# Narrower one-hots in the second column of a strip, and five small moves in the order of work, in a spectral transform with balanced expert assignment

## The chip, the cores and the metric

The kernel runs on one core of a Trainium2 chip. The metric is the time of one execution on the device in microseconds (us). Three runs of the kernel before gave 534.44, 532.58 and 536.25 us, median 534.44. The profile comes from one further execution, whose span from the first to the last instruction is 534.3 us.

## The reference

Two stages follow one another. The first takes the real part of a two-dimensional Fourier transform of every batch; the second sends each of the 19968 rows to one of eight experts, with at most 2496 rows for each, and puts it through that expert's two matrices.

```python
# x: (8, 2496, 256)
X = np.fft.fft(np.fft.fft(x, axis=1), axis=2).real      # -> 19968 rows of 256
logits = rows @ w_gate                                  # 19968 x 8
for idx in np.argsort(-logits.flatten()):               # best (row, expert) pairs first
    tok, e = idx // 8, idx % 8
    if assigned[tok] >= 0 or counts[e] >= 2496: continue
    assigned[tok] = e; counts[e] += 1
for e in range(8):                                      # w1: 256x1024, w2: 1024x256
    out[assigned == e] = np.maximum(rows[assigned == e] @ w1[e], 0) @ w2[e]
```

## The kernel before

A program in which the order of instructions on TensorE (PE), VectorE (DVE), ScalarE (ACT) and GpSimd (POOL) is the order in which the Python code emits them. Four stretches follow each other.

**Load and logits (0 to about 100 us).** Each batch `b` is loaded (`a_t`, and its mirror image `b_t`) and folded on VectorE. Its columns are transposed on TensorE in three groups (`turn_x`), copied to SBUF by ScalarE, multiplied with a gate table (`gate_x`), and put in place (`place_y`).

```python
for b in range(B):
    a_t, b_t = ab.pop(b)
    nc.vector.tensor_tensor(a_t[:, :, :, 1:D], a_t[:, :, :, 1:D], b_t[:, :, ::-1, D - 1:0:-1], op=AL.add)
    nc.vector.tensor_tensor(a_t[:, :, :, 0], a_t[:, :, :, 0], b_t[:, :, ::-1, 0], op=AL.add)
    # ... loads; two more VectorE operations that write zball[b] for the transform ...
    zts[b] = [turn_x(b, pv, 0), turn_x(b, pv, 1)]       # eight transposes each, one copy
    if b > 0:
        gate_x(b - 1, zts.pop(b - 1))
    zts[b].append(turn_x(b, pv, 2))                     # four transposes
    if b > 0:
        low_y = place_y(b - 1)
    # ... tables of sines and cosines ...
low_y()
gate_x(B - 1, zts.pop(B - 1))
place_y(B - 1)()
```

After it the logits of all rows are computed with tables in two halves (`lps`), and the expert with the greatest logit of each row is chosen.

**Transform (about 100 to 172 us).** Forty units, two for each of twenty blocks of 128 x 8 rows, each of ten matmuls into a PSUM bank (`fftps`). A first search for the threshold of each expert (`first_chain`) goes on at the same time on VectorE. `yield` gives the estimated cost of what was emitted, `SYNC` means that a matmul follows which needs VectorE's result; the loop below puts units in between by these estimates. Four times a whole expert's first matrix is turned (`turn_w`).

```python
def turn_w(e, eng=None):
    for j in range(2):
        for fh in range(2):
            wps = big_ps("wps")                         # one of three PSUM banks, shared with fftps
            # two 512-wide matmuls into wps
            take(w1t[e][:, j, fs], wps, eng=eng)        # copy, here on ScalarE
    if e + 2 < E:
        load_w1(e + 2)

def unit():
    cost = next(units, None)
    if cost is not None:
        clock["PE"] += 1.15; clock["D"] += cost; clock["n"] += 1
        if clock["n"] in (18, 22, 28, 34):
            turn_w((18, 22, 28, 34).index(clock["n"]), "A")
            clock["PE"] += 2.0
    return cost is not None
```

A finished block is combined by VectorE into `stage` (`combine`: two additions, then copies on ScalarE and GpSimd, then a write to DRAM).

**Strips.** Rows that are sure of their expert are sorted straight into strips: each call (`sort_call`) takes eight columns of 128 rows as four pairs. A pair fills 24 slots for each of 8 experts (`SW` = 24, `EW` = 8 x 24 = 192). The second column of a pair counts on from where the first one stopped. The one-hots come from VectorE (`sort_mark`), the sort is a matmul.

```python
# in first_strips, t3 = slot in the strip, t1 = expert
nc.vector.tensor_scalar(v_i, in0=v, scalar1=-MARK, scalar2=0.0, op0=AL.add, op1=AL.max)
# ...
nc.vector.scalar_tensor_tensor(has, in0=t3, scalar=float(SW), in1=sure, op0=AL.is_lt, op1=AL.mult)
nc.vector.scalar_tensor_tensor(v, in0=t1, scalar=float(SW), in1=t3, op0=AL.mult, op1=AL.add)
nc.vector.scalar_tensor_tensor(spot, in0=v, scalar=1.0, in1=has, op0=AL.add, op1=AL.mult)

# in sort_mark(n)
for f in range(8):
    nc.vector.tensor_scalar(marks[n][:, f, 0:EW + 1], in0=rampw[:, 0:EW + 1], scalar1=spot[:, c:c + 1],
                            scalar2=None, op0=AL.is_equal)

# in sort_call(n, gs)
for g in gs:
    sps = big_ps("sps")
    for cc in range(2):
        for j2 in range(2):
            nc.tensor.matmul(sps[:, j2 * EW:(j2 + 1) * EW], lhsT=xl[:, 2 * g + cc, j2 * P:(j2 + 1) * P],
                             rhs=pt[:, 2 * g + cc, 0:EW], start=(cc == 0 and j2 == 0),
                             stop=(cc == 1 and j2 == 1))
    take(dst[:, :, 4 * u + g, :], sps[:, 0:2 * EW]...)  # one copy of 384 columns
```

Rows that are not sure, or find no slot, are left over; they are settled later and gathered.

**Experts (about 172 us to the end).** 56 tiles: 40 early ones from the strips (tiles 0 to 39), 16 late ones whose rows GpSimd gathers from DRAM. Each tile has three parts. In a part TensorE computes three (or two) blocks of the hidden layer (`hps`, two matmuls each, copied to `hb` by ScalarE or VectorE) for this tile, and one output block (`ops`, eight matmuls) for the tile before, which GpSimd writes to DRAM by row number. The rest of the assignment (`settle_rest`) is emitted in small steps after each part:

```python
def pace(j):                                            # after every part
    credit[0] = min(credit[0] + 1.9, CREDIT)            # CREDIT = 3.0
    while credit[0] > 0.0 and not placed:
        c = next(todo, "end")
        if c == "end":
            settled(j); return
        if c is SYNC:                                   # a pause: go on after the next part
            return
        credit[0] -= c

def settle_rest():
    yield from settle()                                 # ends in: yield SYNC; transpose of trun on TensorE
    for _ in range(NROUND - 1):
        yield from round_steps(4, 2)
    # ...
    yield from choose_rest()                            # choose(False); yield SYNC; count() on TensorE
    yield from slots(rest, LB)
    # ... then lists of the rows left over, and settled
```

When all is placed, `feed` (in part 1 of each tile) lets the gathers start, spread over the tiles that are left:

```python
while m < len(late) and placed and j >= min(max(placed[0] + 1 + m * (51 - placed[0]) // 15, 0 if m < 8 else 32), 38 + m):
    gather(late[m])                                     # three indirect DMAs issued by GpSimd
    m += 1
```

## Time and profile before

Busy time in some stretches, in us:

| stretch (us) | length | TensorE | VectorE | ScalarE | GpSimd | what runs |
|---|---|---|---|---|---|---|
| 60 to 80 | 20 | 12.29 | 18.73 | 16.84 | 7.35 | last folds |
| 100 to 120 | 20 | 17.70 | 17.90 | 8.47 | 11.10 | transform |
| 120 to 140 | 20 | 16.44 | 15.79 | 11.42 | 6.40 | transform |
| 160 to 180 | 20 | 17.95 | 17.14 | 15.61 | 5.22 | transform to first tile |
| 200 to 220 | 20 | 19.99 | 17.92 | 16.30 | 11.31 | early tiles |
| 300 to 350 | 50 | 49.50 | 31.04 | 31.70 | 27.48 | early tiles, gathers from 328 |
| 400 to 450 | 50 | 50.00 | 25.91 | 26.68 | 38.09 | early and late tiles |
| 500 to 534 | 34 | 23.92 | 11.03 | 11.22 | 22.10 | last tiles, last writes |

In the lines of a timeline that follow, the columns are: start in us, length in us, engine, line of the kernel, operation, what is written and read, its partitions and elements and type, how many in a row, and in brackets the idle time of the engine before it and what ended it. In a line of the stretches they are: the stretch, its length, then busy time and number of instructions of PE (matmuls), PEld (weight loads), DVE, ACT and POOL, the mean granted clock of TensorE as a share of full speed, the share of the DMA engines and their GB/s. GpSimd's busy time covers only part of what an indirect DMA costs it: about 0.97 us of length and 0.30 us of a gap that is there each time.

### The profile page before, as it was taken

The numbers are of one execution on the slowest core, as the hardware profiler recorded it, in microseconds if no ns is written. First come the engines' busy times: TensorE is split into PE (matmuls) and PEld (weight loads), VectorE is DVE, ScalarE is ACT, GpSimd is POOL, SyncE is SP. The second block draws the span as 40 slices with busy tenths as digits, with TensorE's granted clock in tenths as the row PEclk, the third lists the DMA queues.
The fourth block names the chain that finished last, engine by engine and source line by source line (L and its number), as shares of the span: only waits on it lengthen the run. The fifth ranks groups of instructions, "written<-read, shape, count | busy, mean of one in ns | idle before, by whom it ended". The sixth has DMA issues, their size and how long they took to land.

```text
span 534.3 us, 11232 instructions
## 1 busy us (share of the span) xinstructions
PE 471.8 (88%) x4039; PEld 357.7 (67%) x4039; DVE 372.7 (70%) x952; ACT 337.9 (63%) x762; POOL 313.9 (59%) x362
## 2 busy tenths in 40 slices
PE   0567659899789899999899999999999999999983
PEld 0544436776568566777667877777777777777753
DVE  7799994687978969889978757566654555555431
ACT  7879983156368778788767776556555555555531
POOL 7888815253122555555524336777677777777774
PEclk9968898999989999999989999999999999999988
DMA  8999929078578697523322323342222222222221
GB/s 259 317 281 319 310 89 159 2 240 291 140 217 261 161 225 163 137 95 103 99 76 100 99 88 102 113 130 85 82 83 78 79 87 84 79 69 78 77 77 53
DMA packets 35168, 74.62 MB, mean 140 GB/s; under 512 B 6115, under 2 KB 14349, under 8 KB 35104
## 3 DMA queue, kind: packets, MB, share of 16 engines
q0 software_dynamic: 23296, 42.10, 30.2%
q1 hardware_dynamic: 11808, 31.73, 17.7%
q8 instruction: 33, 0.54, 0.4%
q14 instruction: 31, 0.25, 0.2%
HBM read 51.26 MB, written 32.24 MB: 156 GB/s over the span
## 4 chain that ended last, share of the span: by engine, by line
PE 70%; DVE 13%; ACT 9%; issue 4%; DMA 3%; POOL 1%; POOLq 0%; DVEq 0%; ACTq 0%
PE hps L1234 24%; PE ops L1257 24%; PE sps L1098 5%; PE fftps L1038 5%; PE wps L1058 2%; PE tp L285 2%; ACT zt L287 2%; DMA xa<-in_x_dram 2%; PE yps L295 1%; ACT tf L254 1%; POOL out_dram L1261 1%; DVE xa L343 1%; PE inv_ps L766 1%; DVE stage L1022 1%; PE tp L1222 1%
## 5 line engine op out<-in xcount | busy, mean ns | idle before, releaser
L995 ACT ACTIVATE hb<-hps 128x384 bf16<-128x384 f32 (+1 forms) x326 | 146.2, 493 | 50.5 <-PE hps L1234 47.4
L1257 PE MATMUL ops<-w2t,hb 128*128 128x256 bf16 (+1 forms) x1344 | 175.3, 274 | 0.0
L1257 PEld LDWEIGHTS <-hb 128*128 128x128 bf16 (+1 forms) x1344 | 133.3, 100 | 32.6 <-issue 0.5
L1261 POOL DMA_INDIRECT out_dram<-zball,rid x85 | 89.3, 1051 | 82.7 <-ACT zball L995 63.8
L1234 PE MATMUL hps<-xs,zball 128*128 128x384 bf16 x640 | 127.3, 327 | 0.0
L1234 PEld LDWEIGHTS <-zball 128*128 128x128 bf16 x896 | 86.1, 98 | 43.4 <-issue 2.9
L999 DVE TENSOR_SCALAR hb<-hps 128x384 bf16<-128x384 f32 (+1 forms) x122 | 66.3, 549 | 47.2 <-PE hps L1234 39.2
L129 POOL DMA_INDIRECT xb<-in_x_dram,mir_i x40 | 54.3, 1357 | 11.9 <-issue 10.5
L995 ACT ACTIVATE zball<-ops 128x256 f32<-128x256 f32 (+1 forms) x79 | 30.4, 384 | 31.6 <-PE ops L1257 29.0
L1234 PE MATMUL hps<-xt,zball 128*128 128x384 bf16 (+1 forms) x256 | 48.4, 322 | 0.0
L285 PE MATMUL tp<-identf,xa 128*128 128x128 f32 x160 | 27.4, 336 | 20.1 <-issue 9.2
L285 PEld LDWEIGHTS tp<-identf,xa 128*128 128x128 f32 x160 | 23.6, 176 | 27.1 <-issue 10.2
L995 ACT ACTIVATE xs<-sps 128x384 bf16<-128x384 f32 x68 | 30.4, 493 | 16.0 <-PE sps L1098 15.7
L1026 POOL COPY stage<-stage 128x258 bf16<-128x258 bf16 x40 | 17.7, 447 | 36.3 <-DVE stage L1021 33.0
L1098 PE MATMUL sps<-pt,xl 128*128 128x192 bf16 x320 | 33.8, 246 | 0.7 <-DVE pt L1076 0.7
L1076 DVE TENSOR_SCALAR pt<-rampw,spot 128x193 bf16<-128x193 bf16 x160 | 32.5, 298 | 1.6 <-PE inv_ps L766 0.9
L1098 PEld LDWEIGHTS <-xl 128*128 128x128 bf16 x320 | 27.6, 98 | 3.5 <-issue 1.6
L1210 POOL DMA_INDIRECT xg<-t_dram,ids_l x24 | 23.1, 964 | 7.3 <-issue 7.3
L1261 POOL DMA_INDIRECT out_dram<-zball,rows_l x23 | 22.3, 969 | 7.3 <-issue 2.4
L1044 ACT COPY ev<-fftps 128x512 f32<-128x512 f32 x20 | 11.7, 584 | 22.9 <-PE fftps L1038 15.5
L1001 DVE COPY zball<-ops 128x256 f32<-128x256 f32 (+1 forms) x29 | 12.3, 424 | 19.4 <-PE ops L1257 19.4
L1024 ACT ACTIVATE stage<-stage 128x254 bf16<-128x254 bf16 x40 | 15.6, 414 | 13.3 <-DVE stage L1021 11.6
(356 smaller groups left out, 781.1 us busy)
## 6 DMA issues: line engine op xcount, KB each, us to landing
t_dram<-stage SPq DMA_DIRECT2D x20, 512.0 KB
xl<-t_dram SPq DMA_DIRECT2D x20, 512.0 KB
xa<-in_x_dram SPq DMA_DIRECT2D x8, 1024.0 KB
w1raw<-in_moe_w_dram POOLq DMA_DIRECT2D x8, 512.0 KB, 5.3
w2t<-in_moe_w_dram POOLq DMA_DIRECT2D x8, 512.0 KB, 6.3
xa<-in_x_dram SPq DMA_DIRECT2D x8, 224.0 KB
out_dram<-zball,rid POOLq DMA_INDIRECT x85, 2.5
xb<-in_x_dram,mir_i POOLq DMA_INDIRECT x40, 8.0
```

The costliest lines, as they stand in the source:

```text
L129: nc.gpsimd.indirect_dma_start(out=bv[0:n, i, :], out_offset=None, in_=x_pairs, in_offset=bass.IndirectOffsetOnAxis(ap=mir_i[0:n, b * NK + ...
L285: nc.tensor.transpose(tp[:, blk, u, :], pv[:, 4 * c + u, blk * P:(blk + 1) * P], identf)
L995: nc.scalar.activation(dst, src, ACT.Relu if relu else ACT.Copy)
L999: nc.vector.tensor_scalar(dst, in0=src, scalar1=0.0, scalar2=None, op0=AL.max)
L1026: nc.gpsimd.tensor_copy(st[:, :, 1 + q, 0:P + 1], st[:, :, 3 * q, 0:P + 1])
L1038: nc.tensor.matmul(fps[:, :, d0:d1], lhsT=tab[:nv, i, ks], rhs=zball[:nv, b0:b0 + NB, 2 * i + r, d0:d1], start=(i == 0), stop=(i == NK - 1))
L1076: nc.vector.tensor_scalar(marks[n][:, f, 0:EW + 1], in0=rampw[:, 0:EW + 1], scalar1=spot[:, c:c + 1], scalar2=None, op0=AL.is_equal)
L1098: nc.tensor.matmul(sps[:, j2 * EW:(j2 + 1) * EW], lhsT=xl[:, 2 * g + cc, j2 * P:(j2 + 1) * P], rhs=pt[:, 2 * g + cc, 0:EW], start=(cc == 0 ...
L1210: nc.gpsimd.indirect_dma_start(out=xg[0:nr, q, :], out_offset=None, in_=t_dram, in_offset=bass.IndirectOffsetOnAxis(ap=d["ids"](q, nr), ax ...
L1234: nc.tensor.matmul(hps[:, 0:n], lhsT=w1t[d["e"]][:, j2, fc * P:(fc + 1) * P], rhs=d["x"](j2), start=(j2 == 0), stop=(j2 == 1))
L1257: nc.tensor.matmul(ops[0:nr, 0:D], lhsT=d["hid"][:, fc, b0:b0 + nr], rhs=w2t[d["e"]][:, fc, :], start=(fc == 0), stop=(fc == F // P - 1))
L1261: put = nc.gpsimd.indirect_dma_start(out=out, out_offset=bass.IndirectOffsetOnAxis(ap=d["rows"](b0 // P)[0:nr], axis=0), in_=ot[0:nr, :], ...
```

## The change

Six things are changed.

1. The second column of each pair may use slots 8 to 23 only (`SC` = 24 and 16 slots). Its one-hots are 129 instead of 193 wide, its sort matmuls 128 instead of 192. The slot arithmetic is done for each of the two columns by itself. A row of the second column that falls into a slot below 8 is left over.
2. The fold of the last batch is done in three pieces, so that the transposes of the first rows need not wait for all, and `gate_x` of the batch before stands ahead of them. `gate_x` takes the three groups one after the other, so that it can begin with the first.
3. Weight turns are cut into 16 pieces of two matmuls and one copy, one after each of 16 units.
4. A second pause stands in front of the transpose in the first `settle` of the rest,
5. and one more in front of the count in `choose_rest`.
6. The gathers' formula has 50 and 37 in place of 51 and 38.

```diff
+SC = (24, 16)
...
-        for blk in range(2):
-            for c, zt in enumerate(zts):
+        for c, zt in enumerate(zts):
+            for blk in range(2):
...
-        nc.vector.tensor_tensor(a_t[:, :, :, 1:D], a_t[:, :, :, 1:D], b_t[:, :, ::-1, D - 1:0:-1], op=AL.add)
-        nc.vector.tensor_tensor(a_t[:, :, :, 0], a_t[:, :, :, 0], b_t[:, :, ::-1, 0], op=AL.add)
+        for i0, i1 in ((0, 2), (2, 4), (4, NK)) if b == B - 1 else ((0, NK),):
+            nc.vector.tensor_tensor(a_t[:, i0:i1, :, 1:D], a_t[:, i0:i1, :, 1:D], b_t[:, i0:i1, ::-1, D - 1:0:-1],
+                                    op=AL.add)
+            nc.vector.tensor_tensor(a_t[:, i0:i1, :, 0], a_t[:, i0:i1, :, 0], b_t[:, i0:i1, ::-1, 0], op=AL.add)
...
+        if b == B - 1:
+            gate_x(b - 1, zts.pop(b - 1))
         zts[b] = [turn_x(b, pv, 0), turn_x(b, pv, 1)]
-        if b > 0:
+        if 0 < b < B - 1:
             gate_x(b - 1, zts.pop(b - 1))
...
-    def settle():
+    def settle(more=0):
...
-        yield SYNC
+        for _ in range(1 + more):
+            yield SYNC
         bps = misc()
         nc.tensor.transpose(bps[:, 0:P], trun.to_broadcast([P, P]), identf)
...
-        nc.vector.tensor_scalar(v_i, in0=v, scalar1=-MARK, scalar2=0.0, op0=AL.add, op1=AL.max)
+        for cc in range(2):
+            nc.vector.tensor_scalar(by_cols(v_i, cc), in0=by_cols(v, cc), scalar1=2.0 * SEG - (SW - SC[cc]) - MARK,
+                                    scalar2=0.0, op0=AL.add, op1=AL.max)
...
-        nc.vector.scalar_tensor_tensor(has, in0=t3, scalar=float(SW), in1=sure, op0=AL.is_lt, op1=AL.mult)
-        nc.vector.scalar_tensor_tensor(v, in0=t1, scalar=float(SW), in1=t3, op0=AL.mult, op1=AL.add)
-        nc.vector.scalar_tensor_tensor(spot, in0=v, scalar=1.0, in1=has, op0=AL.add, op1=AL.mult)
+        for cc in range(2):
+            hc, sc, vc, a1, a3 = (by_cols(t, cc) for t in (has, spot, v, t1, t3))
+            # the same three operations on one of the two columns, with SC[cc] for SW
...
+        # strip_places: one more addition, which gives the second column its 8 slots back
...
     def choose_rest():
         yield from choose(False)
         yield SYNC
+        yield SYNC
         count()
...
-        yield from settle()
+        yield from settle(1)
...
-            c = b0 * 4 * NK + f * NK + kc
-            nc.vector.tensor_scalar(marks[n][:, f, 0:EW + 1], in0=rampw[:, 0:EW + 1], scalar1=spot[:, c:c + 1],
+            c, w = b0 * 4 * NK + f * NK + kc, E * SC[f % 2] + 1
+            nc.vector.tensor_scalar(marks[n][:, f, 0:w], in0=rampw[:, 0:w], scalar1=spot[:, c:c + 1],
...
-                    nc.tensor.matmul(sps[:, j2 * EW:(j2 + 1) * EW], lhsT=xl[:, 2 * g + cc, j2 * P:(j2 + 1) * P],
-                                     rhs=pt[:, 2 * g + cc, 0:EW], start=(cc == 0 and j2 == 0),
+                    into = sps[:, j2 * EW:(j2 + 1) * EW].rearrange("p (e s) -> p e s", s=SW)
+                    nc.tensor.matmul(into[:, :, SW - SC[cc]:], lhsT=xl[:, 2 * g + cc, j2 * P:(j2 + 1) * P],
+                                     rhs=pt[:, 2 * g + cc, 0:E * SC[cc]].rearrange("p (e s) -> p e s", s=SC[cc]), start=(cc == 0 and j2 == 0),
...
+    TURNS = (*range(15, 23), *range(26, 30), *range(33, 37))
+    pieces = (None for e in range(4) for _ in turn_pieces(e, "A"))
...
-            if clock["n"] in (18, 22, 28, 34):
-                turn_w((18, 22, 28, 34).index(clock["n"]), "A")
-                clock["PE"] += 2.0
+            if clock["n"] in TURNS:
+                next(pieces)
+                clock["PE"] += 0.45
...
-        while m < len(late) and placed and j >= min(max(placed[0] + 1 + m * (51 - placed[0]) // 15, 0 if m < 8 else 32), 38 + m):
+        while m < len(late) and placed and j >= min(max(placed[0] + 1 + m * (50 - placed[0]) // 15, 0 if m < 8 else 32), 37 + m):
```

The cuts leave out the remaining lines of `strip_places`, the views by column, and the generator `turn_pieces`, which has the body of `turn_w` with a `yield` after each copy.

## The prediction

> **What bounds the kernel now.** I read the page first (busy shares, chain by engine), then the busy time by stretches, then the lines of the timeline in which TensorE stood still, then GpSimd's own timeline.
>
> ```profile
> PE 471.8 (88%) x4039; PEld 357.7 (67%) x4039; DVE 372.7 (70%) x952; ACT 337.9 (63%) x762; POOL 313.9 (59%) x362
> ...
> PE 70%; DVE 13%; ACT 9%; issue 4%; DMA 3%; POOL 1%; POOLq 0%; DVEq 0%; ACTq 0%
> ```
>
> TensorE carries 70% of the chain that ended last, and the 13% of DVE are the places where it waits for VectorE. By stretches (second number: TensorE busy):
>
> ```profile
> 80.00:100.00 20.00, 18.02 (x352) 14.05 (x352) 8.19 (x33) 5.49 (x12) 7.24 (x22) 0.91 0.70 107
> ...
> 140.00:160.00 20.00, 17.89 (x136) 13.66 (x135) 15.66 (x47) 10.10 (x23) 4.01 (x9) 0.91 0.54 165
> ...
> 240.00:260.00 20.00, 20.00 (x167) 15.27 (x166) 18.10 (x63) 16.48 (x42) 10.03 (x10) 1.00 0.36 117
> 260.00:300.00 40.00, 36.87 (x315) 27.43 (x314) 32.69 (x107) 28.32 (x70) 16.27 (x17) 0.96 0.27 89
> ```
>
> From 180 us on TensorE is full except for single holes. The holes, and what stands after them, from the timeline (start, length, in brackets the idle time before and its releaser):
>
> ```profile
> 148.33 0.59 PE L1058 MATMUL wps<-w1raw,mt_b 128*128 128x512 bf16 x2 [2.11 <-ACT zball L995]
> 180.05 0.32 PE L690 MATMUL misc<-identf,trun 128*128 128x128 f32 x1 [2.10 <-DVE trun L686]
> 267.62 0.72 PE L601 MATMUL misc<-dd,onesb 128*128 128x128 bf16 x10 [2.74 <-DVE dd L594]
> 269.04 2.13 PE L1234 MATMUL hps<-xs,zball 128*128 128x384 bf16 x6
> 513.26 0.26 PE L1222 MATMUL tp<-identb,xs 96*128 96x96 bf16 x2 [1.45 <-DMA xs<-t_dram,ids_l]
> ```
>
> The first is the third weight turn (`turn_w`), waiting for ScalarE; the second the transpose in `settle`; the third the `count` of `choose_rest`; the last the turn of the last gathered tile. The fourth line shows what a hole costs besides: six matmuls that take 1.14 us elsewhere take 2.13.
>
> GpSimd's timeline shows a second limit:
>
> ```profile
> 387.25 0.97 POOL L1261 DMA_INDIRECT out_dram<-zball,rid  x1 [1.28 <-DVE zball L1001]
> 388.52 0.99 POOL L1210 DMA_INDIRECT xg<-t_dram,ids_l  x1 [0.30 <-issue]
> ...
> 507.50 0.99 POOL L1210 DMA_INDIRECT xs<-t_dram,ids_l  x1 [0.30 <-issue]
> ...
> 528.13 0.93 POOL L1261 DMA_INDIRECT out_dram<-zball,rows_l  x1 [0.30 <-issue]
> ```
>
> From 387.25 to 528.13 there are 111 issues, 1.28 us from one to the next, and only one gap above 0.33 us. So in the last 141 us GpSimd, not TensorE, sets the end. From 328 to 387 it waits for TensorE's results only 2.6 us in all (five gaps). What shortens the time is therefore what brings forward the moment near 387 us (tile 30 or so), and TensorE's work before it.
>
> **What the Trainium skill says.** "TensorE: Matmul & The Clock Gate", section "Wait — 56ns, not 53.3ns?": start to start a matmul takes its columns at 2.4 GHz plus about 2.5 ns, by its figures 82.5 ns at 192 columns and 55.8 at 128. The trace agrees: eight 192-column matmuls of `sort_call` take 0.83 us with a last one of 0.246, so (0.83-0.246)/7 = 83 ns; six 128-column transposes take 0.50 with 0.219, so 56 ns, each with its own weight load. Same page, "What's actually happening": after an idle window the array runs at half clock. The trace agrees in kind: 2.13 us against 1.14 above. Same page, "Step-by-step: what each phase is for": matmuls stay in program order, only weight loads are pulled ahead. That is why a matmul put too early in the program holds up all behind it, and what a pause mends. "VectorE: DVE Perf Modes", section "The perf-mode tier table (the rule you actually need)": a single-source 16-bit op gets up to four elements a cycle. The eight one-hots take 1.53 us, last one 0.298, so 176 ns from one to the next. The slope between 193 and 129 columns is not in this trace; an estimate at two elements per cycle of that page's 0.96 GHz is 64/2/0.96 = 33 ns.
>
> **The change part by part.**
>
> *Last fold and gate.* Now the last fold (2.81 us from 77.09, plus the column at 79.82) must end before the first transpose at 80.09; then transposes, the gate matmuls of the batch before (82.94, 2.56 us), two more transposes, the last gate matmuls (86.57), and the logits start at 90.41. TensorE stood idle 2.28 us before 80.09. In pieces the first 2/5 are there at 77.09 + 1.2 + 0.15 = 78.4, and the gate matmuls of batch 6 move into the hole: they can start at 77.8, when the transposes of batch 5's values end, and run to about 80.2. Then transposes, copies (two of 1.01 us and one of 0.59 on ScalarE) and the last gate matmuls, which by the new order need the third block last: I get their end at 85.5, the copies (0.37 twice), transposes (0.65), cast (0.29) and subtraction (0.33) lead to 87.9. Saved: 90.4-87.9 = 2.5 us, all on the path.
>
> *Weight turns in pieces.* 16 pieces of 1.73/4 = 0.43 us instead of four blocks. The work is the same; the hole of 2.11 us and the slow clock behind it (four groups at 149 to 152 take 0.97, 1.27, 1.29, 1.12 instead of some 0.72) are to go. But the copy waited on ScalarE because ScalarE waited for the stage of a combine, and that combine stood on VectorE behind the long chain of `first_strips` and the first one-hots (till 146.07). In pieces, TensorE meets the same combine a little later: by my walk through the static schedule, unit 26 needs the bank that this combine frees and stands some 2.4 us. Against that, the two searches lose the block ahead of their small matmul (VectorE idle 1.65 and 1.95 us there). I count 1.0 us, well below the 3.8 that the hole suggests.
>
> *Narrow sort.* 160 of the 320 matmuls of `sort_call` go from 192 to 128 columns: 83-56 = 27 ns each. 128 of them lie in tiles 0 to 31: 3.5 us, of which I take 3.2 since some fall after 340 us, where GpSimd has little slack. 32 lie in the transform stage: 0.9 us. Copies out of PSUM stay 384 wide. One-hots: 4 x 33 ns = 0.13 us per call, some 2.6 us of VectorE in all, mostly beside TensorE. Added: four more small VectorE ops in `first_strips` and one in `strip_places`; 0.24 to 0.33 us for 160 elements becomes two of some 0.2, so +0.45 us in the chain; it is in the 1.0 above.
>
> *Pauses.* One in the first `settle`: its transpose comes one part later. TensorE then has eight `sps` (0.6), six `hps` (0.97) and eight `ops` (0.87) to do, 2.4 us against a hole of 2.10: saved 2.1. One in `choose_rest`: together with the first the count moves from tile 13 part 0 to tile 13 part 2, two parts of 1.9 us, while VectorE, full from 257 to 267.6, gets ready about 0.5 later. The hole of 2.74 goes, and with it the slow clock: (2.13-1.14) + (1.56-1.04) + 0.25 for the sort behind it = 1.8. Saved: 4.5.
>
> *Gathers.* With the credit of 1.9 per part, cap 3.0, I walked the generator: before, all is placed at tile 20 part 0 and gathers fall at tiles 21, 23, ... 49, 52; after, at 20 part 2, with gathers at 21, 23, ... 49, 51. Only the last moves, one tile earlier, past three writes (3.85 us). That ends the holes at 511 to 513 us and the slow clock after them, some 4 us of TensorE; but the writes queue on GpSimd to 528 anyway. Saved: the one late gap, 0.3.
>
> Sum: 2.5 + 1.0 + 3.2 + 0.9 + 2.1 + 4.5 + 0.3 = 14.5 us. Such a sum is seldom had whole, since each shift puts a later wait elsewhere; I take five sixths, 12 us: 534.4-12 = 522.4, say 522.5.
>
> **The rivals.** (1) The chain of VectorE stays the limit in the transform stage and in the slots: pieces then bring nothing or lose (4 more ops, a new hole before unit 26), and the count finds VectorE late again. For it: 18.1 of 20 us busy in 240 to 260. Against it: the hole is 2.74, and two parts are 3.8. It would leave 527 to 529. (2) GpSimd is the bound earlier than I think, from 328 on: what TensorE gains between 328 and 387 then vanishes, about 1.2 us of the narrow sort, and with a chain that ends a tile later GpSimd would lose 6 - 3 x 1.28 = 2 us more. It would make 525 to 526. (3) Narrow matmuls are no faster, because weight loads last 98 ns. Against it: 56 ns from one transpose to the next with a load each. It would cost 4.1: 526.5. (4) The other way: the slow clock at 149 goes entirely and the searches run through; then 518 to 519.
>
> **Range and chances.** Certain to me are the fold, the two pauses and the narrow sort, together 13.2, of which I would expect at least 8 to arrive; the pieces may give -1 to +4. That makes 517.5 to 528.0. Two per cent of 534.4 is 523.7, just above my value: faster 0.60, within 0.38, slower 0.02 (only if more tokens were left over than the late tiles take, so that a fallback ran; the slot limit drops few, since 128 tokens over 8 experts seldom leave fewer than 8).
>
> **What would show it.** The logits' first matmul at 87 to 89 us instead of 90.41. No hole above 0.5 us at `settle`'s transpose and at `choose_rest`'s count, and six `hps` at 1.14 behind it. Narrow `sps`: a call's eight in about 0.72 us instead of 0.83. The third turn's hole gone, but one at unit 26 of the transforms. First gather still at tile 21, last one earlier, no wait of the last turn; GpSimd without gaps to the last write, and the end set by it. Wrong would be: first gathers a tile later, GpSimd idle after 400 us, or a new hole of 2 us in the slots.

## The result and the profile after

The changed kernel takes 528.18 us (527.79 to 530.57), the kernel before 535.3 us in the runs beside it: ratio 0.988, 95% interval 0.984 to 0.993. The forecast was 522.5. So 7 us were gained, 1.2% by that ratio, where the sum of the forecast had 14.5 and the forecast itself 12.

The head of the page of the changed kernel (span, busy time by engine) and its chain:

```profile
span 526.0 us, 11245 instructions
...
PE 463.3 (88%) x4039; PEld 351.1 (67%) x4039; DVE 374.1 (71%) x963; ACT 335.1 (64%) x760; POOL 316.0 (60%) x362
...
issue 0%; POOL 0%
POOL out_dram L1285 0%
```

TensorE's busy time fell by 8.5 us and the span of the traced execution by 8.3 (from 534.3), so TensorE's share stayed at 88%. The chain now breaks off at once at GpSimd's last write and says nothing further. The stretches, as for the kernel before (second number: TensorE busy; the last three: granted clock, DMA share, GB/s):

```profile
80.00:100.00 20.00, 15.54 (x350) 13.41 (x350) 11.16 (x38) 5.02 (x12) 7.24 (x22) 1.00 0.70 107
140.00:160.00 20.00, 18.12 (x158) 14.25 (x157) 16.64 (x56) 13.67 (x32) 6.41 (x15) 1.00 0.79 241
240.00:260.00 20.00, 19.44 (x166) 14.84 (x164) 17.80 (x64) 15.55 (x40) 9.41 (x10) 1.00 0.30 108
260.00:300.00 40.00, 39.00 (x343) 28.88 (x341) 33.67 (x111) 30.68 (x78) 19.20 (x18) 1.00 0.30 99
```

The last stretch is fuller than before (39.00 against 36.87), as meant. The third was full and now has a gap of 0.56: something new stands there. The timeline of TensorE names it (start, length; in brackets the idle time before, and its releaser):

```profile
87.27 0.19 PE L457 MATMUL lps_cE<-yhl,hi_cE 128*128 128x64 bf16 x1 [0.74 <-DVE yhl L310]
...
93.81 0.19 PE L457 MATMUL lps_cO<-yhl,hi_cO 128*128 128x64 bf16 x1 [1.53 <-issue]
...
130.71 0.29 PE L845 MATMUL lev_ps<-identf,s_lev 128*128 128x128 f32 x1 [3.07 <-DVE stage L1038]
...
178.00 0.27 PE L696 MATMUL misc<-identf,trun 128*128 128x128 f32 x1
...
197.26 0.16 PE L662 MATMUL misc<-s_many,bdiag 128*128 128x1 bf16 x1 [0.55 <-DVE s_part L656]
...
206.64 0.32 PE L696 MATMUL misc<-identf,trun 128*128 128x128 f32 x1 [1.16 <-DVE trun L691]
...
246.58 0.66 PE L632 MATMUL lt<-identf,lists_x 128*128 128x128 f32 x4 [0.56 <-DVE lists_x L624]
...
267.30 0.72 PE L606 MATMUL misc<-dd,onesb 128*128 128x128 bf16 x10
```

The first `settle` (178.00) and the count of `choose_rest` (267.30) have no bracket any more: both holes that the pauses were to close are closed. But there are holes which the kernel before did not have: 1.53 us inside the logits, with no releaser ("issue"), and 0.55, 1.16, 0.39 and 0.56 in the rounds of the search between the two pauses (`lev_ps` at 130.71 belongs to the transforms).

To see where the gain goes, I take the moment at which the first output block of a tile begins to be copied out of PSUM as that tile's mark, and compare the lengths of the stretches between marks in the two traces (us):

| stretch of TensorE | before | changed | gained | forecast |
|---|---|---|---|---|
| start to the logits' first matmul | 90.41 | 87.27 | 3.1 | 2.5 |
| logits to the transforms' first matmul | 10.12 | 11.82 | -1.7 | 0 |
| transforms to tile 0 | 77.46 | 76.52 | 0.9 | 1.9 |
| tile 0 to 1 (first `settle`) | 8.44 | 6.07 | 2.4 | 2.2 |
| tile 1 to 12 (three rounds) | 78.49 | 81.71 | -3.2 | 1.2 |
| tile 12 to 14 (count) | 19.12 | 15.36 | 3.8 | 4.7 |
| tile 14 to 20 | 42.15 | 41.34 | 0.8 | 0.6 |
| tile 20 to 31 | 66.24 | 65.05 | 1.2 | 1.2 |

From tile 31 to 53 the lead stays at 7.29 us; then the earlier last gather gives TensorE another 4.28. GpSimd's last write is issued 7.46 us earlier. Its timeline near the start of its full stretch and at the end:

```profile
333.06 0.97 POOL L1285 DMA_INDIRECT out_dram<-dd,rid  x1 [1.05 <-ACT dd L1011]
334.34 0.99 POOL L1234 DMA_INDIRECT xg<-t_dram,ids_l  x1 [0.31 <-issue]
...
380.06 0.97 POOL L1285 DMA_INDIRECT out_dram<-zball,rid  x1 [1.05 <-DVE zball L1017]
...
520.67 0.93 POOL L1285 DMA_INDIRECT out_dram<-zball,rows_l  x1 [0.30 <-issue]
```

Behind 333.06 its gap exceeds the regular 0.30 to 0.31 us only twice (0.35 at 344.65 and the line at 380.06).

One thing has to be said of the numbers below: in the groups of `p_` to `f_`, of `e_`, `d1_`, `d3_`, `d4_` and of `g1_` to `g3_` every kernel, the one before too, took some 50 us longer, in the traces taken there all of it after tile 20 (81 to 85 us from tile 20 to 31, where the table has 65 and 66), for a reason that is not known, so that of those runs only what lies before tile 20, the tail behind the last issue, and times inside one group are compared.

### The profile page after: what moved, and what is told of

Same layout as the page of the kernel before. It is cut to its first block, busy times and chain, and to the rows that moved or that the text cites. A ratio compares the mean times of both kernels' runs of the same rounds, so it can differ in the third digit from the quotient of the medians.

```text
span 526.0 us, 11245 instructions
## 1 busy us (share of the span) xinstructions
PE 463.3 (88%) x4039; PEld 351.1 (67%) x4039; DVE 374.1 (71%) x963; ACT 335.1 (64%) x760; POOL 316.0 (60%) x362
## 5 line engine op out<-in xcount | busy, mean ns | idle before, releaser
L1011 ACT ACTIVATE hb<-hps 128x384 bf16<-128x384 f32 (+1 forms) x319 | 142.9, 492 | 53.8 <-PE hps L1258 49.1
L1285 POOL DMA_INDIRECT out_dram<-zball,rid x85 | 91.1, 1072 | 77.5 <-ACT zball L1011 59.8
L1258 PEld LDWEIGHTS <-zball 128*128 128x128 bf16 x896 | 84.6, 98 | 45.4 <-issue 7.4
L1015 DVE TENSOR_SCALAR hb<-hps 128x384 bf16<-128x384 f32 (+1 forms) x129 | 70.2, 549 | 45.1 <-PE hps L1258 35.3
L1011 ACT ACTIVATE zball<-ops 128x256 f32<-128x256 f32 x82 | 31.5, 384 | 32.1 <-PE ops L1281 31.2
L1097 DVE TENSOR_SCALAR pt<-rampw,spot 128x193 bf16<-128x193 bf16 (+1 forms) x160 | 30.8, 285 | 0.1
L1120 PE MATMUL sps<-pt,xl 128*128 128x192 bf16 (+1 forms) x320 | 29.4, 232 | 0.1
L1120 PEld LDWEIGHTS <-xl 128*128 128x128 bf16 x320 | 25.6, 98 | 3.6 <-issue 1.4
L1285 POOL DMA_INDIRECT out_dram<-wa,rid x20 | 19.8, 989 | 6.1 <-issue 2.7
```

What stands on the lines that cost most here:

```text
L1011: nc.scalar.activation(dst, src, ACT.Relu if relu else ACT.Copy)
L1015: nc.vector.tensor_scalar(dst, in0=src, scalar1=0.0, scalar2=None, op0=AL.max)
L1097: nc.vector.tensor_scalar(marks[n][:, f, 0:w], in0=rampw[:, 0:w], scalar1=spot[:, c:c + 1], scalar2=None, op0=AL.is_equal)
L1120: nc.tensor.matmul(into[:, :, SW - SC[cc]:], lhsT=xl[:, 2 * g + cc, j2 * P:(j2 + 1) * P], rhs=pt[:, 2 * g + cc, 0:E * SC[cc]].rearrange("p ...
L1258: nc.tensor.matmul(hps[:, 0:n], lhsT=w1t[d["e"]][:, j2, fc * P:(fc + 1) * P], rhs=d["x"](j2), start=(j2 == 0), stop=(j2 == 1))
L1285: put = nc.gpsimd.indirect_dma_start(out=out, out_offset=bass.IndirectOffsetOnAxis(ap=d["rows"](b0 // P)[0:nr], axis=0), in_=ot[0:nr, :], ...
```

## Experiments

### Where the three rounds lose: four variants of the changed kernel

H1: the pause squeezes the round behind it. H2: VectorE got more copies, because a batch of one-hots is booked at 1.1 instead of 1.3 (`busy["D"]`, by which copies are shared out between VectorE and ScalarE; the changed kernel has this number too, though the list of the change leaves it out). H3: the hole in the logits comes from the weights loaded at that time.

```diff
# a1_no_first_pause
-        yield from settle(1)
+        yield from settle()
# a2_book_1_3
-        busy["D"] += 1.1
+        busy["D"] += 1.3
# a3_second_pause: a pause more in the settle of the first of the three rounds
+            yield from round_steps(4, 2, 1 if r == 0 else 0)
# a4_w2_later: the first two load_w2 behind the logits
```

> The changed kernel without the pause in the first settle (everything else as changed). Theory H1 (the pause shortens the next round of the search in TensorE's time, so its waits find VectorE late, and that gives back 3.3 us between tiles 2 and 12): the hole of about 2.1 us at the transpose of settle comes back at tile 1 (the lead over the kernel before at the output blocks of tile 1 falls from 4.75 to about 2.4), but the holes of 1.16 us at the next settle and the other new ones in tiles 3 to 12 vanish, so that the lead at tile 12 is about 3.5 instead of 1.5; the count then comes one part earlier and finds VectorE late by about 1 to 2 us. Total within 1.5 us of the changed kernel. Theory H2 (the loss comes from more PSUM copies on VectorE, because a batch of one-hots is now booked at 1.1 instead of 1.3): the lead falls between tiles 2 and 12 all the same, from about 2.4 to -0.8, and the total is about 2 us above the changed kernel.

527.31 us, against 528.18 of the changed kernel. The stretch from tile 1 to 12 falls from 81.71 to 78.32, its new holes are gone; in return the hole at `settle` is back with 2.32 us, and TensorE's clock fell behind it, so that tile 0 to 1 took 10.09 us. H1's picture holds, in tile 1 to 12 more fully than expected. The count itself no longer waits; the waits that were expected there, 0.46, 0.32 and 0.52 us, stand in the slots behind it. H2's picture does not hold: with the same booking of 1.1 the loss is gone. The whole time says nothing here: 0.9 us lie inside the spread of the runs (526.27 to 531.42).

> The changed kernel with one number put back: a batch of one-hots booked on VectorE at 1.3 instead of 1.1, so that fewer PSUM copies are given to VectorE. H2: VectorE's copies of hidden units fall from 129 towards 122, the holes between tiles 2 and 12 go, the lead over the kernel before at tile 12 rises from 1.5 to 4 or more, total 2 to 3 us lower. H1: the holes stay where they are within 0.3 us each, the lead at tile 12 stays 1 to 2, total within 1 us of the changed kernel.

529.42 us. VectorE's copies of hidden units go from 129 to 121 (122 before the change), but the holes stay where they were: 0.55, 1.17, 0.37 and 0.63 us; tile 1 to 12 takes 82.07. H2 falls.

> The changed kernel with one pause more, in the settle of the first of the three further rounds, which had the new hole of 1.16 us at 206.64. H1: that hole goes, and the lead at tile 4 is 1 to 1.2 us higher than in the changed kernel; later rounds come one part later, so the holes at tiles 6 to 12 change place; total 0.5 to 2 us lower. If what matters is VectorE's total work up to the count and not one wait, the hole comes back in the next rounds and the lead at tile 12 stays at 1.5 within 0.5.

528.89 us. The hole of 1.16 is gone, and a new one of 1.53 us stands at the third `settle` and one of 0.48 at the fourth. Tile 1 to 12 takes 81.34. A pause moves the hole to the next round: the second half of the expectation.

> The changed kernel with the first two loads of w2 (0.5 MB each) issued behind the logits instead of ahead of them. H3 (TensorE's own instructions come late while 2 MB of weights are loaded): the hole of 1.53 us in the middle of the logits, behind which the profile shows no wait, goes; the first matmul of the transforms comes at 97.6 instead of 99.1; total 1 to 1.5 us lower if the gain is kept. If the hole has to do with the logits alone, it stays at 1.5 us.

The hole in the logits is gone: from their first matmul to the transforms 10.13 us instead of 11.82. H3 holds in this, that the loads cause the hole. But the total is 528.42, and the transforms to tile 0 take 78.32 us instead of 76.52: VectorE waits 2.14 us at 114.11 for a store to free its tile ("DMA t_dram<-stage"), and TensorE 1.14 at 115.45 for VectorE. That the loads, which now run at this time, hold up the store is likely, since the wait is not there when they are moved further (below).

### Each part alone, put into the kernel before

```diff
# p_pauses_alone
-        yield SYNC
+        for _ in range(1 + more):
+            yield SYNC            # settle(1) in settle_rest, one more SYNC in choose_rest
# n_narrow_alone: SC = (24, 16), the slots, the one-hots and the matmuls of sort_call
# w_pieces_alone: turn_pieces, TURNS
# f_fold_alone: the last fold in three pieces, the order of the gate
```

The whole times were 585.02 us (pauses), 588.47 (narrow sort), 586.90 (pieces) and 585.82 (fold), and 586.62 for the kernel before, which ranged from 578.34 to 592.97. By these the narrow sort alone made the kernel 0.5% slower (interval 0.1 to 1.0%) and the pauses 0.4% faster (0.2 to 0.7%); as they hold the 50 us behind tile 20, they do not show what a part is worth.

> The kernel before with the two pauses alone. T0 (the terms of the forecast hold, each by itself): 6.6 us less than before, the holes of 2.1 at settle and 2.7 at the count gone, and no new ones. T1 (VectorE's own work between the first settle and the count sets when the count can start, so TensorE's time saved at settle is lost again in the rounds): the two holes go, but new holes of 2 to 3 us in sum stand between tiles 1 and 12, the lead over the kernel before at tile 12 is 0 +- 0.7, and only the count's part stays, 3 to 4 us less in all.

The two holes go: tile 0 to 1 takes 6.13 instead of 8.44, tile 12 to 14 15.95 instead of 19.12. But tile 1 to 12 takes 82.51 instead of 78.49. From tile 0 to tile 20 the pauses bring 148.2 - 145.7 = 2.5 us, not 6.6. T1 is right in kind, and too mild: the lead won at `settle` is not only gone at tile 12 but 1.7 us below zero. TensorE's timeline of that run shows what stands in the rounds:

```profile
201.96 0.16 PE L657 MATMUL misc<-s_many,bdiag 128*128 128x1 bf16 x1 [0.55 <-DVE s_part L651]
...
211.36 0.32 PE L691 MATMUL misc<-identf,trun 128*128 128x128 f32 x1 [1.14 <-DVE trun L686]
...
251.90 0.33 PE L627 MATMUL lt<-identf,lists_x 128*128 128x128 f32 x1 [0.63 <-DVE lists_x L619]
```

With one more of 0.36, these are the holes of the changed kernel, to 0.1 us. So they belong to the pauses, not to the narrow sort, the pieces or the booking. They make 2.7 us; 1.2 more is TensorE's busy time (79.60 instead of 78.43), which was not followed up.

> The kernel before with the narrow sort alone. T0: 4.1 us less (0.9 in the transforms, 0.108 per tile to tile 31). T1: from tile 1 to tile 12 the lead grows by 0.4 us at most instead of 1.2, or falls, and the hole at the count grows by what TensorE had won before it (from 2.7 to 4 us); from tile 13 to 31 it grows by 0.108 per tile as forecast; in all 1.5 to 2.5 us less.

Tile 1 to 12 in the windows view of the kernel before and of this run, and the stretch from tile 20 to 31 before and after the change:

```profile
186.43:264.92 78.49, 78.43 (x643) 57.30 (x642) 67.87 (x216) 63.75 (x155) 42.66 (x40) 1.00 0.60 140
...
326.19:392.43 66.24, 66.24 (x594) 51.35 (x592) 40.29 (x110) 38.33 (x85) 48.00 (x50) 1.00 0.32 103
```

```profile
185.28:263.61 78.33, 78.00 (x643) 56.25 (x642) 67.92 (x217) 62.96 (x153) 42.55 (x39) 1.00 0.60 140
```

```profile
320.09:385.14 65.05, 65.05 (x594) 50.16 (x592) 39.82 (x112) 38.22 (x86) 47.91 (x50) 1.00 0.32 105
```

Both stretches are eleven tiles with the same matmuls per tile in the sort. From tile 20 to 31 the changed kernel is 1.19 us shorter, 11 x 0.108, and none of its other parts touches TensorE's work there. From tile 1 to 12 the narrow sort gives 0.16, though TensorE is full in both but for 0.06 and 0.33 us. What happens is seen at one call: the eight `sps`, the four `hps` behind them, and the next `ops`, in tile 10 before and with the narrow sort, and in tile 24 after the change:

```profile
248.46 0.83 PE L1098 MATMUL sps<-pt,xl 128*128 128x192 bf16 x8
249.12 0.89 PE L1234 MATMUL hps<-xs,zball 128*128 128x384 bf16 x4
249.85 1.03 PE L1257 MATMUL ops<-w2t,hb 128*128 128x256 bf16 x8
```

```profile
247.30 0.72 PE L1109 MATMUL sps<-pt,xl 128*128 128x192 bf16 x8
247.85 0.95 PE L1245 MATMUL hps<-xs,zball 128*128 128x384 bf16 x4
248.64 1.04 PE L1268 MATMUL ops<-w2t,hb 128*128 128x256 bf16 x8
```

```profile
339.82 0.72 PE L1120 MATMUL sps<-pt,xl 128*128 128x192 bf16 x8
340.38 0.81 PE L1258 MATMUL hps<-xs,zball 128*128 128x384 bf16 x4
341.03 1.04 PE L1281 MATMUL ops<-w2t,hb 128*128 128x256 bf16 x8
```

In tile 10 the `sps` end 0.11 us earlier (0.55 from start to start instead of 0.66), and the four `hps` take 0.06 longer (0.79 instead of 0.73). In tile 24 they take 0.65. The code has three PSUM banks for `sps` and `hps` until the placement is done, and a fourth after it (`swap_ps`): with three, TensorE that comes sooner may find the bank not yet copied out. That this is the reason is argued from the code and not shown; no run changed the number of banks. Neither theory had it: the lead does not grow in the rounds (T1), but the hole at the count did not grow either, it stayed at 2.73.

Most of the 1.6 us that this run gains from tile 12 to 14 is not the narrow sort's. After the same hole as in the kernel before, the next matmuls were much less slow:

```profile
266.31 0.72 PE L602 MATMUL misc<-dd,onesb 128*128 128x128 bf16 x10 [2.73 <-DVE dd L595]
...
267.42 1.33 PE L1245 MATMUL hps<-xs,zball 128*128 128x384 bf16 x6
```

Six `hps` in 1.33 us, where the kernel before took 2.13 behind 2.74 us of idle time. And that gain is lost again at tile 19, where TensorE waits for VectorE's one-hots, 2.35 us in this run and 0.50 in the kernel before:

```profile
320.56 0.80 PE L1109 MATMUL sps<-pt,xl 128*128 128x192 bf16 x8 [2.35 <-DVE pt L1086]
```

```profile
321.91 0.87 PE L1098 MATMUL sps<-pt,xl 128*128 128x192 bf16 x8 [0.50 <-DVE pt L1076]
```

So from tile 0 to 20 the narrow sort alone brings only 0.5 us. What T1 says of the rounds is seen here behind the count: TensorE came sooner, and VectorE did not. The changed kernel has no hole at this place.

> The kernel before with the weight turns in pieces alone. T0: the transform stage is 1.0 us shorter, total 1 us less. T1: the transform stage is 0.5 to 2 us shorter, but what TensorE wins there meets VectorE at the first settle (hole there 2.1 plus the win), total the same within 0.7 us.

From the first transform to tile 0 it takes 76.25 us. The hole of 2.11 at the third turn is gone, and 3.08 stand at `lev_ps` (1.29 before) and 1.14 at unit 26, much as in the changed kernel (3.07 and 1.34). Its lead at tile 0 is kept unchanged to tile 20, hole at `settle` included (2.11), so it does not meet VectorE there, against T1. What the pieces gain is not to be had from these runs: the run of the fold alone has the same program as the kernel before in this stretch and takes 75.80 us, the kernel before 77.46. Behind the third turn, after the same hole of 2.1, the next four groups of `fftps` take 0.71 to 0.72 us each there and 0.97 to 1.29 in the kernel before; this slow clock makes nearly all of the 1.66 between them, and no smaller gain shows in single traces.

> The kernel before with the last fold in pieces and the new order of the gate alone. T0: the logits start 2.5 us earlier and the total is 2.5 us less. The three further runs of the changed kernel showed the moved gate matmuls at half clock (3.5 us instead of 1.92) and the hole of 1.5 us within the logits, behind which no wait stands: if both are the rule, the transforms start 0 to 0.5 us earlier only, and the total is 0 to 0.7 us less.

The logits start at 88.79, and 1.51 us are lost in the hole within them; the transforms start at 100.59, against 100.53 in the trace of the kernel before. The second case of the expectation. The gate matmuls keep their clock here, but not always. Before the gate matmuls, the transposes of the third block; in this run, and in the run with the second pause:

```profile
77.86 0.66 PE L285 MATMUL tp<-identf,xa 128*128 128x128 f32 x4 [0.89 <-ACT zt L287]
...
79.62 1.92 PE L295 MATMUL yps<-zt,g_sb 128*32 128x512 f32 x12
```

```profile
76.61 0.66 PE L286 MATMUL tp<-identf,xa 128*128 128x128 f32 x4 [1.32 <-ACT zt L288]
...
78.45 3.47 PE L296 MATMUL yps<-zt,g_sb 128*32 128x512 f32 x12
```

The twelve matmuls moved into the hole take 1.92 us in fourteen of the sixteen runs that have the fold, and 3.47 and 3.61 in two. So one trace does not tell what the fold is worth. Over all runs, the logits' first matmul comes at 90.41, 92.64, 89.89 and 89.53 without it (mean 90.6), and at 87.0 to 89.2 in the sixteen with it (mean 88.1).

### Taking the losses back, and what ends the run

```diff
# c1_round_moved_whole (behind the transpose of the paused settle)
-        yield 0.2
+        yield 0.2 + 1.9 * more
# c2_w2_at_unit_21 (the two load_w2 of the last batch, moved into unit())
+            if clock["n"] == 21:
+                load_w2(wts[0])
+                load_w2(wts[0])
# c3_four_writes_less (in down, ahead of the write)
+        if b0 == 2 * P and d.get("m", 99) < 4:
+            return
```

The first two of these take 527.24 and 527.37 us. Against the 528.18 of the changed kernel that is less than the spread of the runs of each (526.27 to 529.11 and 526.52 to 528.63), so that what they are worth is read from the stretches.

> The changed kernel with 1.9 of the budget booked behind the paused first settle, so that all that follows it moves one part later and keeps its distances (in the changed kernel the second settle stays in tile 4, part 2, though the first came a part later). H1 (the pause squeezes the next round, and its waits find VectorE late): the new holes behind the pause, 0.55 and 1.16 us at tiles 3 and 4 and 0.39 and 0.56 later, go, the lead over the kernel before grows by 2.3 at settle and stays within 0.7 of that to tile 12 instead of falling by 3.2; the count then stands at tile 14 part 0 and all is placed one tile later, so that the first gather falls at tile 22: GpSimd may lose up to 2 us again. Total 1 to 3 us below the changed kernel. T1 (VectorE has no time to spare up to the count): holes of 2 to 3 us in sum stand there again, lead at tile 12 falls by 2.5 or more, total not lower.

In TensorE's timeline the hole at the second `settle` has shrunk from 1.16 to 0.65, and one of 0.95 has come at the third:

```profile
207.71 0.32 PE L696 MATMUL misc<-identf,trun 128*128 128x128 f32 x1 [0.65 <-DVE trun L691]
234.82 0.32 PE L696 MATMUL misc<-identf,trun 128*128 128x128 f32 x1 [0.95 <-DVE trun L691]
```

From the logits' start to tile 20 it takes 231.50 us instead of 232.82: 1.3 better. The lead of 4.8 us at tile 1 is still 4.82 at tile 6 (3.04 in the changed kernel), and 2.32 at tile 12. Another 1.0 of the gain comes at the count (tile 12 to 14 in 14.35 us, 15.36 in the changed kernel). So H1 is right for the first round behind the pause, and is not the whole: in the later rounds the loss comes back, as T1 said.

> The changed kernel with the first two loads of w2 issued only in the middle of the transforms (unit 21, about 130 us), where the DMA engines are at a third of their time. H3: as with the loads just behind the logits, no hole in the logits (1.4 to 1.8 us saved), but now no wait of a stage for its store at 114 us either; the first matmul of tile 0 comes 1.3 to 1.8 us earlier than with the logits' hole, and the total is 1 to 1.5 us below the changed kernel. If the transforms are held by VectorE anyway, the lead is gone by tile 0 and the total is the same.

From the logits' start to tile 20 it takes 231.75 us, 1.1 better, with no hole in the logits and no wait for a store. That the loads make the hole is settled. How they do it can be inferred from the queues that carry instructions. Packets between 91 and 94 us in the changed kernel (columns: queue, packets, MB, summed packet time as a share of the DMA engines' time, which can pass 100%):

```profile
q0 software_dynamic: 1009, 0.51, 125.9%
q8 instruction: 1, 0.02, 2.0%
```

and between 87 and 91 us with the loads moved:

```profile
q0 software_dynamic: 108, 0.19, 25.4%
q8 instruction: 1, 0.02, 2.1%
```

The logits start at 87.27 and at 87.03. With the loads moved, the next packet of instructions runs before 91; in the changed kernel the stretch from 87 to 91 has none, it comes after 91, and TensorE stands from 92.28 to 93.81. All thirteen runs that started the logits before 90 us with the loads in their old place have the hole (1.40 to 1.84 us), two of them without the fold; the five with the loads moved and the two that started after 90 (90.41 and 92.64) do not. In the thirteen this packet starts 3.9 to 4.4 us behind the logits' first matmul, in the seven others 1.4 to 2.6. The profile does not say whose instructions the packet brings, so the late packet as the cause is inferred. The Trainium skill says in "Runtime: NRT & Kernel Launch", section "Instruction fetch mechanics", that a sequencer fetches its next block of 16 KiB through a DMA queue of its own while it works on the current one, and that the cost is mostly hidden. The packets here agree in size (16384 bytes, 0.02 MB in the view), and they stand in a queue of their own; but in these thirteen runs TensorE stood for 1.40 to 1.84 us.

> The changed kernel with four of its 168 writes left out: the third block of tiles 40 to 43 is computed and copied out of PSUM, but not written (so 4 x 128 or 96 rows of the output stay unwritten). E1 (GpSimd, one issue each 1.28 us without gaps, sets the end): total 4 to 5.1 us less (4 x 1.28 = 5.1), TensorE's end unchanged. E2 (TensorE's chain sets the end): total the same within 0.5 us.

528.56 us: nothing gained, against E1. GpSimd did issue its last write 4.1 us earlier, at 516.55, but in the traces the span fell only from 526.0 to 524.6. TensorE's last matmuls began at 510.98 (510.96 in the changed kernel). What follows them is the jump over the conditional block behind the last tile. In the view of that line of the run (duration, first and last start):

```profile
L1378 POOLq EVENT_SEMAPHORE  x6: 17/30/43, 519.1 to 521.7; - x6
...
L1378 PEldq EVENT_SEMAPHORE  x2: 51/51/51, 519.1 to 519.2; - x2
...
L1378 PEldq COMPARE_BRANCH  x1: 4258/4258/4258, 514.7 to 514.7; - x1
```

TensorE's sequencer takes 4.26 us for the jump (3.50 in the changed kernel's trace, 3.74 before), and only then meets the others, at 519.1. That is a second limit, 1.4 us behind GpSimd's. In the kernel before it was the first one. There the jump was late:

```profile
L1352 PEldq COMPARE_BRANCH  x1: 3742/3742/3742, 526.2 to 526.2; - x1
```

It ended at 530.0 (526.24 + 3.74), 0.9 us behind the end of GpSimd's last issue (529.06), and the tail from there to the end of the span was 5.24 us; in the changed kernel the jump ended at 518.0, 3.6 us ahead of GpSimd's last issue, and the tail was 4.39. So, by these traces, some 0.85 us of the gain in the span came from TensorE's earlier end, and the prediction's reading that GpSimd alone set the end was off by as much.

```diff
# d3_no_block_behind: the conditional block for left-over tokens is left out (this input does not enter it)
# d4_no_block_four_less, g3_no_block_four_less: that, and the four writes less
# d1_both_mended, g1_both_mended: c1 and c2 together
# g2_all_rounds_moved: that, and settle(1) with its 1.9 in the next two rounds as well
```

> The changed kernel once more, as the measure for the other three: 528 us, ratio 0.985 to 0.990. Where TensorE's clock falls to half at the moved gate matmuls, the logits start at 89 instead of 87.3 us.

> The changed kernel with both mendings: w2's first loads at unit 21, and 1.9 of the budget booked behind the first settle. H1 and H3 as separate causes: TensorE's lead over the changed kernel is 1.3 to 1.5 at tile 0 and 2.5 to 3 at tile 31, total 2.3 to 2.9 us less than the changed kernel beside it. If one takes the place of the other (the earlier start only meets VectorE in the slots): 1.0 to 1.5 less. If a limit behind the last tile sets the end: TensorE is earlier, the total the same within 0.5.

> The changed kernel without the conditional block behind the last tile (the further rounds and tiles for tokens that found no place, which this input does not enter), so without the jump over it. E3 (after TensorE's last matmul the jump and what it must fetch take 9 to 10 us, only 1.4 us less than GpSimd's issues and their landing): with all writes GpSimd sets the end, the total falls by 0 to 1.5 us. If the jump adds to the end of GpSimd: 2.5 to 4 us less.

> As the run without the block behind the last tile, and four writes less besides (the third block of tiles 40 to 43 is not written). E3: now GpSimd is the only limit, and the four writes bring 3.5 to 5.1 us (4 x 1.28 = 5.1, less what GpSimd waits for the last tiles) against the run with all writes. If TensorE's last tile itself is the limit, they bring under 1 us again.

In this group the kernel before took 586.50 us and the changed one only 0.6% less, not 1 to 1.5%. The times were 581.82 us (changed kernel), 580.38 (both mended), 578.21 (no block behind) and 574.92 (that, and four writes less). Without the block the tail behind GpSimd's last issue is 2.8 and 2.6 us instead of 6.2 in the changed kernel beside it, and the time 3.6 lower: more than E3 said, probably because here TensorE ended only 2.8 us ahead of the end of GpSimd's last issue and not 7 as in the first trace, so that the jump was the limit. The four writes then bring 3.3 us. This supports E3; with intervals of 1.3 to 1.8% in these runs it does not measure it.

> The changed kernel with both mendings, timed again. H1 and H3 as separate causes: span 523.2 to 523.7 (526.0 of the changed kernel, less 1.4 for the loads and 1.2 for the round moved whole), time 525 to 526 us, ratio to the kernel before 0.981 to 0.984. If the gains do not add: 527 us, 0.986.

> As the first, and the settles of the next two rounds have a pause with 1.9 of the budget behind it as well. H1: the holes of 0.65 and 0.96 us go and no new ones of more than 0.5 us come between tiles 1 and 12; lead over the kernel before at tile 12 some 2 us higher than with the first settle's alone; the placement ends 2 parts later (tile 21, part 2), so that the first gather stands at tile 22, where GpSimd and the turn of tile 40 have slack; total 1 to 2.5 us less than the first run. T1 (VectorE has nothing to spare): new holes of 1.5 us or more in sum, total the same.

> The changed kernel without the block behind the last tile and with four writes less. E3 (after TensorE's last matmul the jump and its fetches are the second limit): 4 us or more below the changed kernel's 528.2, of which 1 to 2 are the shorter tail and the rest the four writes. If the four writes are hidden by something else, the last tile itself: 1 to 2 us less.

Both mended: 230.18 and 230.67 us from the logits' start to tile 20 in the two runs, against 232.82 and 233.08 of the changed kernel. That is 2.2 to 2.9, and 1.3 + 1.1 was to be added: the two losses are separate. Four more traces have the changed kernel's program up to tile 20 and took 232.92, 233.38, 233.91 and 235.16, the last with a slower clock behind the hole in the logits. The whole time was 581.07 and 580.38, against 581.82 of the changed kernel; what it is where the late tiles run through was not measured. With all rounds moved 232.95, worse by 2.3 to 2.8, and TensorE's timeline has new holes:

```profile
233.32 0.16 PE L660 MATMUL misc<-s_many,bdiag 128*128 128x1 bf16 x1 [1.11 <-DVE s_part L654]
...
259.88 0.16 PE L660 MATMUL misc<-s_many,bdiag 128*128 128x1 bf16 x1 [1.11 <-DVE s_part L654]
...
265.71 0.32 PE L694 MATMUL misc<-identf,trun 128*128 128x128 f32 x1 [1.58 <-DVE trun L689]
```

They are T1's. But VectorE is busy only 64.92 of 81.29 us from tile 1 to 12, so "nothing to spare" is too simple: the waits depend on what else stands ahead of each step in VectorE's order. Which work that is, stays open; less work on VectorE in these tiles was not tried. The third run: 576.27 us, tail 2.6, as its twin above.

## Why the prediction was wrong, by its own steps

Of the 7.2 us between the sum of 14.5 and the 7.3 by which TensorE led, 4.4 are missing in the three rounds, 1.7 in the logits, 1.0 in the transforms and 0.9 at the count; the start gave 0.6 more than forecast.

**The pauses (2.1 + 4.5): the step that failed.** Both holes went as said, and six `hps` behind the count take 1.14. But the step counted the holes that are closed, and none that are opened. A pause does not give VectorE time; it lets TensorE run ahead by a part, and the budget that places the three rounds then packs the next round, from the first `settle` to the second, into ten parts instead of eleven. New holes of 2.7 us stand in the rounds, and the stretch from tile 1 to 12 grows by 4.0. By itself the pair brought 2.5 us of 6.6. Of the 4.5 at the count, 1.8 were for the slow clock behind the hole, and one of the four traces with the same hole shows that this cost is not always there.

**The narrow sort (3.2 + 0.9): right for the instruction, wrong for the place.** Eight `sps` take 0.72 us, as forecast, and from tile 20 on the 27 ns per matmul arrive in full. From tile 1 to 12 only 0.16 of 1.19 us arrive: there TensorE, though full, is paced by something else, which stays open. I read "TensorE 20.00 of 20.00" as "shorter matmuls are a shorter stretch". The one-hots' estimate was too high as well: eight take 1.46 us instead of 1.53, so 0.07 and not 0.13 less.

**Fold and gate (2.5): right, with a loss behind it that had no term.** 90.6 to 88.1 in the mean is 2.5. But 1.4 to 1.8 us are given back in the logits, which now start earlier against the loads of the weights.

**Pieces (1.0):** the hole moved from the third turn to unit 26, as foreseen (1.14 to 1.34 us, 2.4 forecast), and to `lev_ps` (3.1), which was not; the gain is smaller than the 1.7 us by which the clock alone moves this stretch, so it is neither shown nor refuted.

**Gathers (0.3): right for GpSimd, short at the end.** GpSimd's last 111 issues take 140.61 us instead of 140.88. TensorE's chain ends 4.3 us sooner for the earlier last gather, and of that some 0.85 reach the end, since in the kernel before the jump behind TensorE was the last to finish. That GpSimd sets the end holds for the changed kernel, by about 1.4 us.

**The rivals.** The first one, with its 527 to 529, came nearest: VectorE was the limit, but in the rounds, and not at the count where it expected the wait. That the number fits is partly luck. The second (GpSimd the limit from 328 on) did not come: the 1.2 us of tiles 20 to 31 reached GpSimd's last write. The third came in effect between tiles 1 and 12, but not through weight loads, since eight `sps` did take 0.72 us there. The fourth did not come. Of the slow clock I had the kind right and took it for a fixed price.

## What to carry to other kernels

A pause in one engine's program order closes the hole at that wait, but it shifts everything placed by a budget behind it: walk the steps up to the next fixed point, and count the waits that open there. Where an engine is full, look once at what follows the instruction that is to become shorter: if the next group grows by about what was saved, something other than the engine paces it, perhaps a buffer. And before moving a stage earlier, see what the DMA engines do at the new time: here a stage without a transfer of its own lost 1.4 to 1.8 us to loads that were under way.

## What the hardware showed unasked

Waits without a releaser ("issue") of 1.4 to 1.8 us stood once in the logits of thirteen of the fifteen runs in which the loads of `w2` (1 MB) were issued ahead of them, and in none of the five in which they were issued later; with the wait, a packet of instructions started 3.9 to 4.4 us behind the logits' first matmul, without it 1.4 to 2.6. The slow clock after idle time is not a fixed price: behind holes of 2.74 and 2.73 us, six equal matmuls took 2.13 and 1.33 us, and the same twelve gate matmuls took 1.92 or 3.47. A jump over a large block that is not entered cost TensorE's sequencer 3.5 to 4.4 us, and the tail behind GpSimd's last issue was 2.6 to 2.8 us without that block and 4.4 to 7.1 with it.
